# Half-width stationary operands by turns, two half steps to a burst, in a fused linear attention and two MoE layers

## The chip, the cores and the metric

One core of a Trainium2 chip runs the whole program in one launch. The metric is the time of one execution on the device in microseconds (us). The engines are TensorE (PE for its matmuls, PEld for its weight loads), VectorE (DVE), ScalarE (ACT), GpSimd (POOL) and SyncE (SP), which here issues the DMAs.

## The reference, cut to what matters

```python
# q, k, v: (4, 8, 576, 64); omega: (128, 64)
def phi(x):
    h = einsum('bhsd,md->bhsm', x, omega) - sum(x * x) / 2
    return exp(h - max(h)) / sqrt(m)
q_p, k_p = phi(q * scale), phi(k * scale)
kv  = einsum('bhsm,bhsd->bhmd', k_p, v)      # per batch and head: 128 x 64
z   = sum(k_p, axis=2)                       # per batch and head: 128
num = einsum('bhsm,bhmd->bhsd', q_p, kv)
den = einsum('bhsm,bhm->bhs', q_p, z) + 1e-6
x   = num / den                              # 2304 tokens x 512
x   = (silu(x @ w_gate) * (x @ w_val)) @ w_out          # d_ff 1536
out = x, and for the tokens that a skip score picks: x + gate * relu(x @ w1[e]) @ w2[e], 8 experts
```

## The kernel before, in words

The 2304 tokens are 18 tiles of 128 and 9 groups of 256. The attention is cut into half steps: 36 of kind "k" (they add to `kv` and `z`) and 36 of kind "q" (they make the numerators). A half step takes four (token tile, head) blocks. Two neighbouring tiles of one batch make a wide step (`w == 2`) of two heads each; tile 4 and tile 13 straddle two batches (576 tokens are 4.5 tiles) and are taken alone, in two runs of 64 tokens. The list `steps` has the k steps of the first nine tiles, the q steps of groups 0 to 3, then the k steps of the other nine tiles, and the q steps of groups 4 to 8.

Each half step begins in `phi` (line 301): two transposes (`tp`, line 329), the projection (`pj`: lines 345 to 347 up to step `first`, line 373 after it), sums and maxima on DVE, and four exponentials on ACT (line 396) into `pexp`, of which there are three buffers. A k step then runs four matmuls with `pexp` as the stationary operand, 128 columns wide, and 65 columns of `v` with a column of ones as the moving one (line 433, result `kvps` in PSUM). A q step transposes `pexp` (line 473), copies that to `qt` (line 477; three buffers), and runs four matmuls with `qt` stationary and 65 columns of `kv` moving (line 483, result `nm`). In the tiles 4 and 13 line 433 runs on 64 rows, twice, and line 483 on 64 columns, first all of one half and then all of the other. All of these are float32, and each stands in the trace as two pairs of a weight load and a matmul.

After `nm` come a reciprocal and a product on DVE (lines 492 to 497), two transposes (`tx`, line 510) and a split into a high and a low part (`xth`, `xtl`). `ups(g)` (line 669) multiplies a whole group by the first MoE's weights, `downs(g)` (lines 712 to 714) by the last of them. These two are the large part of TensorE's work, and they also fill it between the steps of the attention.

The order on every engine is made when the program is built. `Order` holds generators that each yield their next operation with an engine, a planned cost in ns, what it waits for, and which buffer slots it takes; the operation that can start first comes next, and the priority decides between equals. On the chip each engine runs its list in that order. Slots: six PSUM banks `a`, three `pexp`, three `g` (for `qt`), two buffers for `v` in the later half of the attention.

Of the kernel before, what the change touches and what calls it, by code (L numbers as in the profile page):

```python
# [9 lines left out]
F32 = mybir.dt.float32  # L10
# [40 lines left out]
def op(eng, ns, *after, take=()):  # L51

    return eng, ns, after, take


class Order:
# [26 lines left out]
    def rel(self, name, t, what=None):  # L83
        self.n += 1
        self.slots[name].append((t, self.n, what))
# [47 lines left out]
def tile_attn_moe_moe2(  # L133
# [90 lines left out]
    def runs(i, w):  # L224

        t0 = i * P
        if w == 2:
            yield 0, P, t0 // S, t0 % S
            return
        done = 0  # L230
        while done < P:
            b, s = divmod(t0 + done, S)
            n = min(P - done, S - s)
            yield done, n, b, s
            done += n

    def half_of(w, c):
        return c // 2 if w == 2 else c

    def head_of(w, c, u):  # L240

        return 2 * (c % 2) + u // 2 if w == 2 else u
# [34 lines left out]
    def give(name, buf, t):  # L277

        if late[name] and any(buf is b for b in aa + va):
            n_extra[0] -= 1  # L280
            if not n_extra[0]:
                rel("W", t)
        else:
            rel(name, t, buf)
# [36 lines left out]
    def phi(j, box, prio):  # L321

        yield op(None, 0, C["A", j])
        a = C["A", j].buf
        c_sq = od.add(square(a, C["A", j], box), prio)
        t = yield op("pe", 218, C["A", j], take=("a",))
        tp = ps_a.tile([P, 2, P], F32, tag="a", name="tp")
        for i in range(2):
            nc.tensor.transpose(tp[:, i, :], a[:, i, :], ident)
        od.add(give_later("A", a, t, c_sq))  # L330
        c_s = None
        if j < first:
            t = yield op("act", 264, t, take=("th",))
            tt = sp.tile([P, HH, P], F32R, tag="th", name="th")
            th, tl = tt[:, 0:2, :], tt[:, 2:4, :]
            nc.scalar.copy(th, tp)
            t = yield op("dve", 335, t)
            nc.vector.tensor_tensor(out=tl, in0=tp, in1=th.bitcast(F32), op=ALU.subtract)
            rel("a", t)
            c_s = od.add(sumsq(c_sq, box), prio)  # L340
            t = yield op("pe", 654, t, take=("a",))
            pj = ps_a.tile([P, HH, M], F32, tag="a", name="pj")
            for i in range(2):
                o = pj[:, 2 * i:2 * i + 2, :].rearrange("p h m -> p (h m)")
                nc.tensor.matmul(o, lhsT=th[:, i, :], rhs=omh, start=True, stop=False)
                nc.tensor.matmul(o, lhsT=tl[:, i, :], rhs=omh, start=False, stop=False)
                nc.tensor.matmul(o, lhsT=th[:, i, :], rhs=oml, start=False, stop=True)
            C["pj", j].t = t
            rel("th", t)
        else:  # L350

            ta, tl = [], []
            for r in range(2):
                ta.append((yield op("act", 264, t, take=() if r else ("th",))))
                if not r:
                    tt = sp.tile([P, 2, 2, P], F32R, tag="th", name="th")
                nc.scalar.copy(tt[rows[r], :, r, :], tp[rows[r]])  # L357
            for r in range(2):
                tl.append((yield op("dve", 335, ta[r])))
                nc.vector.tensor_tensor(  # L360
                    out=tt[rows[1 - r], :, r, :], in0=tp[rows[r]], in1=tt.bitcast(F32)[rows[r], :, r, :],
                    op=ALU.subtract,
                )
            rel("a", tl[1])
            c_s = od.add(sumsq(c_sq, box), prio)
            yield op(None, 0, take=("pexp",))
            box["pexp"] = sp.tile([P, HH, M], F32, tag="pe", name="pexp", bufs=3)
            td = []
            for i in range(2):
                t = yield op("pe", 218, *tl, C["omx"], take=("a",))  # L370
                pj = ps_a.tile([P, 2, 2, M], F32, tag="a", name="pj")
                for r in range(2):
                    nc.tensor.matmul(
                        pj[:, r].rearrange("p x m -> p (x m)"), lhsT=tt[:, i, r, :], rhs=omh, start=True, stop=True
                    )
                if i:
                    rel("th", t)
                td.append(od.add(halves(box, i, pj, t), prio))
            t = yield op(None, 0, *td)
            pj = box["pexp"]  # L380
        t = yield op("dve", 598, t, c_s)
        mx, mh, bi = (box["st"][:, i, :] for i in range(1, 4))
        nc.vector.tensor_reduce(out=mx, in_=pj, axis=AX.X, op=ALU.max)
        t = yield op("dve", 73, t, c_s)
        nc.vector.scalar_tensor_tensor(
            out=mh, in0=box["ssq"], scalar=-0.5 * scale * scale, in1=mx, op0=ALU.mult, op1=ALU.add
        )
        t = yield op("dve", 73, t)
        nc.vector.scalar_tensor_tensor(  # L389
            out=bi, in0=box["ssq"], scalar=-0.5 * scale * scale, in1=mh, op0=ALU.mult, op1=ALU.subtract  # L390
        )
        t = yield op("act", 1004, t, take=("pexp",) if j < first else ())
        if j < first:
            box["pexp"] = sp.tile([P, HH, M], F32, tag="pe", name="pexp", bufs=3)
        for h in range(HH):
            nc.scalar.activation(out=box["pexp"][:, h, :], in_=pj[:, h, :], func=ACTF.Exp, bias=bi[:, h:h + 1])  # L396
        if j < first:
            rel("a", t)
        rel("small", t)
        return t  # L400
# [14 lines left out]

    kvt = {}

    def kstep(j, prev, prio):
        _, i, w, c = steps[j]
        hf = half_of(w, c)  # L420
        box = {}
        t = yield from phi(j, box, prio)
        for off, n, b, s in runs(i, w):
            head = opens[b, hf] == j
            t = yield op("pe", 856, t, C["V", j], prev, take=("a",) if head else ())
            vt = C["V", j].buf
            if head:
                kvt[b, hf] = ps_a.tile([P, HH, D + 2], F32, tag="a", name="kvps")
            shares[b, hf] -= 1
            last = not shares[b, hf]  # L430
            for u in range(4):
                r = u % 2
                nc.tensor.matmul(
                    kvt[b, hf][:, head_of(w, c, u), r:r + D + 1], lhsT=box["pexp"][off:off + n, u, :],
                    rhs=vt[off:off + n, u // 2, r * (D + 1):(r + 1) * (D + 1)],
                    start=head and u == 0, stop=last, skip_group_check=True,
                )
            if last:
                od.add(kv_end(b, hf, t), 0, C["kv", b, hf])
        rel("pexp", t)  # L440
        give("V", vt, t)

    def kv_end(b, hf, t):

# [17 lines left out]
            C["xT", g].t = od.now  # L462

    def qstep(j, prio):
        _, i, w, c = steps[j]
        hf = half_of(w, c)
        part = list(runs(i, w))
        box = {}
        t = yield from phi(j, box, prio)
        t = yield op("pe", 436, t, take=("a",))  # L470
# [5 lines left out]
        qt = gp.tile([P, HH, P], F32, tag="g", name="qt")  # L476
        (nc.vector.tensor_copy if od.eng == "dve" else nc.scalar.copy)(qt, tq)
        rel("a", t)
        t = yield op("pe", 856 * len(part), t, *[C["kv", r[2], hf] for r in part], take=("a",))
        nm = ps_a.tile([P, HH, D + 1], F32, tag="a", name="nm")  # L480
        for off, n, b, s in part:
            for u in range(4):
                nc.tensor.matmul(
                    nm[off:off + n, u, :], lhsT=qt[:, u, off:off + n], rhs=kvs[b][hf][:, head_of(w, c, u), :],
                    start=True, stop=True,
                )
        rel("g", t)
        C["num", j].t = t
        t = yield op("dve", 69, t, take=("small",))
        dn = sm.tile([P, 2, HH], F32, tag="dn", name="dn")  # L490
        de, rd = (dn[:, i, :].rearrange("p (h o) -> p h o", o=1) for i in range(2))
# [31 lines left out]
    def attention():  # L523

        prev = Cell(0.0)
        live = []
        for j, (kind, i, _, _) in enumerate(steps):
            live = [c for c in live if c.t is None]
            if len(live) >= (MAXA if j < first else MAXB):
                yield op(None, 0, live[0])  # L530
                live.pop(0)
            yield op(None, 0, C["A", j], *([C["xT", i // 2]] if kind == "q" else []))
            prio = P_ATT if j < first else P_ATT2
            if kind == "k":
                prev = od.add(kstep(j, prev, prio), prio)
                live.append(prev)
            else:
                live.append(od.add(qstep(j, prio), prio, C["x", j]))
        for c in live:
            yield op(None, 0, c)  # L540

# [1059 lines left out]
```

## Time and profile before

| what | value |
|---|---|
| time before, median of 3 runs (lowest, highest) | 850.65 us (848.59, 850.86) |
| the profiled execution, its own time | 846.94 us |
| its span, first to last instruction | 844.7 us |
| TensorE busy with matmuls | 822.8 us, 97% |
| VectorE, ScalarE, GpSimd busy | 517.5, 446.0, 215.9 us |
| granted TensorE clock, mean | 0.995 of full speed |

The profile is of one execution. Busy times are unions: an engine counts once however many of its instructions are in progress. TensorE's matmuls overlap in the records, so that the price of a burst is read from the start of its first matmul to the start of the next one behind it, and not from the durations.

### The profile page before, as it was taken

What the parts mean: (1) busy time and instruction counts of PE and PEld (TensorE: products, weight loads), DVE (VectorE), ACT (ScalarE), POOL (GpSimd) and SP (SyncE); (2) the same over time, 40 slices, a digit from 0 to 9 for tenths busy, and PEclk for the clock granted to TensorE, in tenths of its full rate; (3) what the DMA queues carried; (4) which work ended last, traced back from release to release, by engine and by line L of the source; (5) the groups of instructions that cost most, each with busy time, mean ns of one, the idle gap of its engine ahead of it and who ended that gap; (6) DMA issues with size and microseconds to landing.
All of it is one profiled execution on the core that took longest, in us unless ns stands there. A gap on an engine that the chain in (4) does not pass through costs nothing. (4 is left out here: it accounts for less than half of the span.)

```text
span 844.7 us, 17205 instructions
## 1 busy us (share of the span) xinstructions
PE 822.8 (97%) x6221; PEld 778.4 (92%) x6221; DVE 517.5 (61%) x1477; ACT 446.0 (53%) x1162; POOL 215.9 (26%) x288
## 2 busy tenths in 40 slices
PE   9999999999999999999999999999999999999993
PEld 8989999999999899999999999999999999999993
DVE  7898777538877762652652651651475767846761
ACT  5897776437767662632632631631355447735560
POOL 4331231223222211211211212232151033342231
PEclk9999999999999999999999999999999999999997
DMA  6856862011222300200200200100185378657640
GB/s 165 234 169 192 249 201 76 1 57 31 53 66 54 95 14 1 70 7 1 75 3 1 75 2 1 63 1 1 52 236 153 117 230 262 218 171 243 200 129 31
DMA packets 77294, 84.46 MB, mean 100 GB/s; under 512 B 19550, under 2 KB 54494, under 8 KB 77200
## 3 DMA queue, kind: packets, MB, share of 16 engines
q1 hardware_dynamic: 73840, 76.23, 29.0%
q0 software_dynamic: 3360, 7.04, 2.8%
q8 instruction: 51, 0.84, 0.4%
q14 instruction: 43, 0.35, 0.1%
HBM read 71.48 MB, written 13.27 MB: 100 GB/s over the span
## 5 line engine op out<-in xcount | busy, mean ns | idle before, releaser
L669 PE MATMUL u<-xth,W 128*128 128x256 f32 x1728 | 247.1, 286 | 0.2 <-DVE h L690 0.2
L669 PEld LDWEIGHTS u<-xth,W 128*128 128x128 f32 x1728 | 225.3, 190 | 5.6 <-DVE h L690 0.4
L697 POOL TENSOR_TENSOR hl<-h,hh 128x256 fp32r<-128x256 f32 x108 | 82.9, 767 | 340.3 <-ACT hh L695 340.1
L669 PE MATMUL u<-xtl,W 128*128 128x256 f32 x864 | 138.8, 283 | 0.0
L669 PEld LDWEIGHTS u<-xtl,W 128*128 128x128 f32 x864 | 119.1, 192 | 0.0
L687 DVE SCALAR_TENSOR_TENSOR h<-h,u 128x256 f32<-128x256 f32 x108 | 45.3, 419 | 113.0 <-ACT h L685 112.4
L695 ACT CAST hh<-h 128x256 fp32r<-128x256 f32 x108 | 43.7, 405 | 116.3 <-DVE h L690 115.8
L690 DVE TENSOR_TENSOR h<-h,u 128x256 f32<-128x256 f32 x108 | 45.3, 419 | 75.5 <-PE u L669 74.8
L712 PE MATMUL y<-W,hh 128*128 128x512 f32 x216 | 87.4, 405 | 0.0
L685 ACT ACTIVATE h<-u 128x256 f32<-128x256 f32 x108 | 41.2, 382 | 83.2 <-PE u L669 81.2
L713 PE MATMUL y<-W,hh 128*128 128x512 f32 x216 | 85.1, 394 | 0.0
L714 PE MATMUL y<-W,hl 128*128 128x512 f32 x216 | 84.5, 391 | 0.0
L1107 DVE TENSOR_TENSOR W<-raw,W 128x512 fp32r<-128x512 f32 x107 | 72.6, 709 | 11.0 <-ACT W L1105 9.7
L1147 PE MATMUL hp<-xgt,W 128*128 128x288 f32 x546 | 76.2, 297 | 0.3 <-DVE W L1170 0.3
L1147 PEld LDWEIGHTS hp<-xgt,W 128*128 128x128 f32 x546 | 73.7, 188 | 0.9 <-DVE W L1170 0.5
L1105 ACT CAST W<-raw 128x512 fp32r<-128x512 f32 x112 | 65.1, 624 | 5.4 <-DMA raw<-in_moe_w_dram 5.3
L396 ACT ACTIVATE pexp<-pexp,st 128x128 f32<-128x128 f32 x184 | 58.8, 391 | 13.3 <-DVE st L389 13.0
L312 POOL TENSOR_TENSOR sq<-a 128x256 f32<-128x256 f32 x54 | 34.2, 632 | 72.8 <-DVE st L318 50.5
L1185 PE MATMUL ym<-W,W 128*128 128x288 f32 x168 | 52.1, 310 | 0.0
L360 DVE TENSOR_TENSOR th<-tp,th 64x256 fp32r<-64x256 f32 x92 | 38.9, 422 | 19.8 <-ACT th L357 17.7
L1187 PE MATMUL ym<-W,W 128*128 128x288 f32 x168 | 49.5, 295 | 0.0
L1186 PE MATMUL ym<-W,W 128*128 128x288 f32 x168 | 49.5, 295 | 0.0
(217 smaller groups left out, 1521.5 us busy)
## 6 DMA issues: line engine op xcount, KB each, us to landing
raw<-in_moe_w_dram SPq DMA_DIRECT2D x64, 512.0 KB, 4.7
scratch<-in_moe_w_out_dram SPq DMA_DIRECT2D x11, 511.8 KB, 3.9
scratch<-in_moe_w_gate_dram SPq DMA_DIRECT2D x11, 511.0 KB, 4.6
scratch<-in_moe_w_val_dram SPq DMA_DIRECT2D x11, 511.0 KB, 4.1
x2s<-x SPq DMA_DIRECT2D x9, 512.0 KB, 2.6
out_dram<-x SPq DMA_DIRECT2D x9, 512.0 KB, 4.0
a<-in_q_dram SPq DMA_DIRECT2D x26, 128.0 KB, 2.2
a<-in_k_dram SPq DMA_DIRECT2D x22, 128.0 KB, 2.3
```

Source lines behind the costliest of these rows:

```text
L396: nc.scalar.activation(out=box["pexp"][:, h, :], in_=pj[:, h, :], func=ACTF.Exp, bias=bi[:, h:h + 1])
L669: nc.tensor.matmul(ps, lhsT=W[fc][:, 2 * n + wi, c * P:(c + 1) * P], rhs=x[:, c, :], start=(a == 0 and c == 0), stop=(a == 2 and c == 3),)
L697: nc.gpsimd.tensor_tensor(out=hl, in0=h, in1=hh.bitcast(F32), op=ALU.subtract)
L712: nc.tensor.matmul(y[n], lhsT=hh[:, s], rhs=W[fc][:, 4, :], start=(fc == 0), stop=False)
L713: nc.tensor.matmul(y[n], lhsT=hh[:, s], rhs=W[fc][:, 5, :], start=False, stop=False)
L714: nc.tensor.matmul(y[n], lhsT=hl[:, s], rhs=W[fc][:, 4, :], start=False, stop=(fc == NFC - 1))
L1105: nc.scalar.copy(blk(m, b, 0), raw[:, j, :])
L1107: (nc.vector if od.eng == "dve" else nc.gpsimd).tensor_tensor(out=blk(m, b, 1), in0=raw[:, j, :], in1=blk(m, b, 0).bitcast(F32), op=ALU.su ...
L1147: nc.tensor.matmul(hp[:, 0:TS], lhsT=blk(m, (fc // 4) * 4 + c, wi)[:, fs], rhs=m2["xt"][xi][:, c, :], start=(a == 0 and c == 0), stop=(a = ...
L1185: nc.tensor.matmul(y, lhsT=wh, rhs=hh, start=(fc == 0), stop=False)
L1186: nc.tensor.matmul(y, lhsT=wl, rhs=hh, start=False, stop=False)
L1187: nc.tensor.matmul(y, lhsT=wh, rhs=hl, start=False, stop=(fc == 7))
```

## The change

Three things change, all in the attention.

First, every 65-column matmul with a stationary operand of 128 columns becomes two, of columns 0 to 63 and 64 to 127 (`rows` holds the two slices), which write partitions 0 to 63 and 64 to 127 of the same PSUM tile. The two stand next to each other, so that the halves come by turns. In tiles 4 and 13 the k matmuls, cut in row halves already, are cut in columns as well, and the q matmuls get the order by turns.

Second, half steps get a mate: two k steps next to each other of one half of the heads, or two q steps of one tile or pair of tiles. The first of the two stops behind its `pexp` (k) or its `qt` (q) and keeps the buffer; the second issues the matmuls of both in one burst. Of 36 k half steps 32 have a mate; all 36 q half steps have one. What follows `nm` becomes a generator of its own (`numer`), started for both.

Third, the planner is told of it: one operation of 1250 ns for a burst of two half steps, or 800 for one, and `pexp` buffers are taken in the order of the steps (`C["px", j]`).

```diff
+    mate = {j: j for j in range(len(steps))}
+    for j in range(1, len(steps)):
+        (kind, i, w, c), (kind2, i2, w2, c2) = steps[j - 1:j + 1]
+        if mate[j - 1] == j - 1 and kind == kind2 and (half_of(w, c) == half_of(w2, c2) if kind == "k" else i == i2):
+            mate[j - 1], mate[j] = j, j - 1
...
     def kstep(j, prev, prio):
         t = yield from phi(j, box, prio)
-        for off, n, b, s in runs(i, w):
-            t = yield op("pe", 856, t, C["V", j], prev, take=("a",) if head else ())
...
+        C["ft", j].t, C["ft", j].buf = t, box["pexp"]
+        if mate[j] > j:
+            return
+        both = sorted({j, mate[j]})
+        t = yield op(
+            "pe", 1250 if len(both) == 2 else 800, *[C[x, n] for x in ("ft", "V") for n in both], prev,
+            take=("a",) * sum(r[-1] for n in both for r in parts[n]),
+        )
+        for n in both:
...
             for u in range(4):
                 r = u % 2
-                nc.tensor.matmul(
-                    kvt[b, hf][:, head_of(w, c, u), r:r + D + 1], lhsT=box["pexp"][off:off + n, u, :],
+                for off, num, b, _, head in parts[n]:
+                    for m in rows:
+                        nc.tensor.matmul(
+                            kvt[b, hf][m, head_of(w, c, u), r:r + D + 1], lhsT=pexp[off:off + num, u, m],
...
     def qstep(j, prio):
+        C["qt", j].t, C["qt", j].buf = t, qt
+        if mate[j] > j:
+            return
...
+            for u in range(4):
+                for m, b in at:
+                    nc.tensor.matmul(
+                        nm[m, u, :], lhsT=qt[:, u, m], rhs=kvs[b][half_of(w, c)][:, head_of(w, c, u), :],
+                        start=True, stop=True,
+                    )
+            od.add(numer(n, nm, t), prio, C["x", n])
```

TensorE's order at the first bursts of k steps, before (`x4` counts the kernel's matmuls; `v_103`, `v_104` and `extra` are buffers of v, `a_105`, `a_106` and `extra` of k):

```order
L347 MATMUL pj<-oml,th 128x256
L433 MATMUL kvps<-v_104,pexp 128x65 x4
L329 MATMUL tp<-ident,extra 128x128 x2
L329 MATMUL tp<-ident,a_105 128x128 x2
L433 MATMUL kvps<-extra,pexp 128x65 x4
L329 MATMUL tp<-ident,a_106 128x128 x2
L433 MATMUL kvps<-extra,pexp 128x65 x4
L345 MATMUL pj<-omh,th 128x256
```

The same place now:

```order
L347 MATMUL pj<-oml,th 128x256
L452 MATMUL kvps<-v_103,pexp 64x65 x8
L452 MATMUL kvps<-v_104,pexp 64x65 x8
L329 MATMUL tp<-ident,a_105 128x128 x2
L345 MATMUL pj<-omh,th 128x256
L346 MATMUL pj<-omh,th 128x256
L347 MATMUL pj<-oml,th 128x256
L345 MATMUL pj<-omh,th 128x256
L346 MATMUL pj<-omh,th 128x256
L347 MATMUL pj<-oml,th 128x256
L452 MATMUL kvps<-extra,pexp 64x65 x16
```

The matmuls of two half steps stand together, twice as many and half as wide, and a projection stands ahead of the second burst that stood behind it.

TensorE's order at the first q steps, before:

```order
L473 MATMUL tq<-ident,pexp 128x128 x8
L510 MATMUL tx<-ident,xx 128x128 x2
L483 MATMUL nm<-kv_1_108,qt 128x65 x4
L510 MATMUL tx<-ident,xx 128x128 x2
L329 MATMUL tp<-ident,extra 128x128 x2
L473 MATMUL tq<-ident,pexp 128x128 x4
L483 MATMUL nm<-kv_1_108,qt 128x65 x4
L510 MATMUL tx<-ident,xx 128x128 x2
L483 MATMUL nm<-kv_0_107,qt 128x65 x4
L473 MATMUL tq<-ident,pexp 128x128 x4
L345 MATMUL pj<-omh,th 128x256
```

The same place now:

```order
L490 MATMUL tq<-ident,pexp 128x128 x8
L512 MATMUL nm<-kv_0_107,qt 64x65 x16
L490 MATMUL tq<-ident,pexp 128x128 x4
L512 MATMUL nm<-kv_1_108,qt 64x65 x16
L544 MATMUL tx<-ident,xx 128x128 x2
L512 MATMUL nm<-kv_0_107,qt 64x65 x16
L544 MATMUL tx<-ident,xx 128x128 x2
L329 MATMUL tp<-ident,extra 128x128 x2
L544 MATMUL tx<-ident,xx 128x128 x4
```

Three bursts now stand within six rows, with no projection among them: those of the next steps have moved ahead of this place.

## Rows read from the trace of the kernel before

**Rows 1.** The page: span; busy us of each engine (share), x instructions.
```profile
span 844.7 us, 17205 instructions
PE 822.8 (97%) x6221; PEld 778.4 (92%) x6221; DVE 517.5 (61%) x1477; ACT 446.0 (53%) x1162; POOL 215.9 (26%) x288
```

**Rows 2.** Stretches, us: length, busy time by engine (x instructions), clock, DMA share, GB/s.
```profile
0.00:45.00 45.00, 42.85 (x352) 40.96 (x352) 35.59 (x127) 33.03 (x106) 17.07 (x41) 1.00 0.73 201
45.00:62.20 17.20, 15.36 (x125) 13.73 (x124) 17.20 (x59) 17.20 (x50) 5.95 (x6) 1.00 0.53 161
62.20:85.00 22.80, 22.80 (x178) 21.98 (x178) 20.13 (x48) 17.89 (x43) 3.37 (x4) 1.00 0.60 185
85.00:566.00 481.00, 480.05 (x3627) 449.90 (x3626) 281.76 (x870) 249.99 (x680) 109.53 (x149) 1.00 0.17 53
566.00:800.00 234.00, 231.42 (x1717) 221.79 (x1716) 143.47 (x339) 113.00 (x253) 69.81 (x78) 1.00 0.53 168
```

**Rows 3.** PE's waits from 85 to 566: us in total, times, longest.
```profile
PE rk L822 <- DVE th L360: 0.3, 1, 0.3
```

**Rows 4.** Instruction groups of PE, 0 to 85: busy us, mean ns, idle before.
```profile
L433 PE MATMUL kvps<-extra,pexp 128*128 128x65 f32 x80 | 10.1, 270 | 0.5 <-ACT pexp L396 0.5
L483 PE MATMUL nm<-kv,qt 128*128 128x65 f32 x64 | 8.3, 273 | 0.3 <-ACT qt L477 0.2
L433 PE MATMUL kvps<-v,pexp 128*128 128x65 f32 x48 | 6.1, 270 | 0.0
L433 PE MATMUL kvps<-extra,pexp 64*128 64x65 f32 x32 | 4.4, 278 | 0.0
```

**Rows 5.** The same view, 85 to 566.
```profile
L483 PE MATMUL nm<-kv,qt 128*128 128x65 f32 x192 | 24.5, 271 | 0.0
L433 PE MATMUL kvps<-v,pexp 128*128 128x65 f32 x128 | 16.3, 270 | 0.0
L433 PE MATMUL kvps<-v,pexp 64*128 64x65 f32 x32 | 4.4, 278 | 0.0
L483 PE MATMUL nm<-kv,qt 128*64 128x65 f32 x64 | 3.9, 227 | 0.0
```

**Rows 6.** PE in order of time, a burst of 128 columns: start, length (us).
```profile
66.72 1.00 PE L483 MATMUL nm<-kv,qt 128*128 128x65 f32 x8
67.53 0.37 PE L669 MATMUL u<-xth,W 128*128 128x256 f32 x1
```

**Rows 7.** PE in order of time, a burst on 64 rows.
```profile
35.70 0.28 PE L347 MATMUL pj<-oml,th 128*128 128x256 f32 x1
35.91 1.10 PE L433 MATMUL kvps<-extra,pexp 64*128 64x65 f32 x8
36.95 0.38 PE L345 MATMUL pj<-omh,th 128*128 128x256 f32 x1
```

**Rows 8.** PE in order of time, the burst of 64 columns of tile 4.
```profile
140.92 0.52 PE L669 MATMUL u<-xtl,W 128*128 128x256 f32 x3
141.37 0.97 PE L483 MATMUL nm<-kv,qt 128*64 128x65 f32 x16
142.27 0.33 PE L748 MATMUL tpr<-ident,x 128*128 128x128 f32 x1
```

**Rows 9.** Weight loads of line 483 in progress (x) in stretches of 0.12 us.
```profile
141.42:141.54 0.12, 0.12 (x4) 1.00 0.00 0
...
141.66:141.78 0.12, 0.12 (x8) 1.00 0.00 0
141.78:141.90 0.12, 0.12 (x8) 1.00 0.00 0
...
66.84:66.96 0.12, 0.12 (x3) 1.00 0.00 0
```

**Rows 10.** Group 4's last transposes; matmuls of line 669 by then (x).
```profile
L510 PE MATMUL tx<-ident,xx x8: 271/272/277, 304.9 to 315.3; 128*128 128x128 f32 x8
...
0.00:315.50 315.50, 134.83 (x1021) 1.00 0.37 111
```

More of the change, by code (lines that the diff above doesn't have):

```diff
@@ L365, in phi @@
             c_s = od.add(sumsq(c_sq, box), prio)
-            yield op(None, 0, take=("pexp",))
+            yield op(None, 0, *([C["px", j - 1]] if j else []), take=("pexp",))
+            C["px", j].t = 0.0
             box["pexp"] = sp.tile([P, HH, M], F32, tag="pe", name="pexp", bufs=3)
@@ L391, in phi @@
         )
-        t = yield op("act", 1004, t, take=("pexp",) if j < first else ())
+        t = yield op("act", 1004, t, *([C["px", j - 1]] if 0 < j < first else []), take=("pexp",) if j < first else ())
         if j < first:
+            C["px", j].t = 0.0
             box["pexp"] = sp.tile([P, HH, M], F32, tag="pe", name="pexp", bufs=3)
@@ L416, in tile_attn_moe_moe2 @@
     kvt = {}
+    mate = {j: j for j in range(len(steps))}
[3 more added lines that the diff above has]
+            mate[j - 1], mate[j] = j, j - 1
     def kstep(j, prev, prio):
-        _, i, w, c = steps[j]
-        hf = half_of(w, c)
         box = {}
         t = yield from phi(j, box, prio)
-        for off, n, b, s in runs(i, w):
-            head = opens[b, hf] == j
-            t = yield op("pe", 856, t, C["V", j], prev, take=("a",) if head else ())
[L426 to L430, printed above, removed]
+        C["ft", j].t, C["ft", j].buf = t, box["pexp"]
+        if mate[j] > j:
+            return
+        both = sorted({j, mate[j]})
+        parts = {n: [(*r, opens[r[2], half_of(*steps[n][2:])] == n) for r in runs(*steps[n][1:3])] for n in both}
+        t = yield op(
[3 more added lines that the diff above has]
+        for n in both:
+            _, _, w, c = steps[n]
+            hf = half_of(w, c)
+            vt, pexp = C["V", n].buf, C["ft", n].buf
+            for _, _, b, _, head in parts[n]:
+                if head:
+                    kvt[b, hf] = ps_a.tile([P, HH, D + 2], F32, tag="a", name="kvps")
+                shares[b, hf] -= 1
@@ L431, in kstep @@
             for u in range(4):
                 r = u % 2
-                nc.tensor.matmul(
-                    kvt[b, hf][:, head_of(w, c, u), r:r + D + 1], lhsT=box["pexp"][off:off + n, u, :],
[L435 to L441, printed above, removed]
+                for off, num, b, _, head in parts[n]:
+                    for m in rows:
+                        nc.tensor.matmul(
+                            kvt[b, hf][m, head_of(w, c, u), r:r + D + 1], lhsT=pexp[off:off + num, u, m],
+                            rhs=vt[off:off + num, u // 2, r * (D + 1):(r + 1) * (D + 1)],
+                            start=head and u == 0, stop=not shares[b, hf], skip_group_check=True,
+                        )
@@ L443, in kv_end @@
+            for _, _, b, _, _ in parts[n]:
+                if not shares[b, hf]:
+                    od.add(kv_end(b, hf, t), 0, C["kv", b, hf])
+            rel("pexp", t)
+            give("V", vt, t)
     def kv_end(b, hf, t):
@@ L464, in qstep @@
     def qstep(j, prio):
-        _, i, w, c = steps[j]
-        hf = half_of(w, c)
-        part = list(runs(i, w))
         box = {}
@@ L478, in qstep, with numer @@
         rel("a", t)
-        t = yield op("pe", 856 * len(part), t, *[C["kv", r[2], hf] for r in part], take=("a",))
-        nm = ps_a.tile([P, HH, D + 1], F32, tag="a", name="nm")
-        for off, n, b, s in part:
-            for u in range(4):
[L483 to L488, printed above, removed]
+        C["qt", j].t, C["qt", j].buf = t, qt
+        if mate[j] > j:
+            return
+        both = sorted({j, mate[j]})
+        t = yield op(
+            "pe", 1250 if len(both) == 2 else 800, *[C["qt", n] for n in both],
+            *[C["kv", r[2], half_of(*steps[n][2:])] for n in both for r in runs(*steps[n][1:3])],
+            take=("a",) * len(both),
+        )
+        for n in both:
+            _, i, w, c = steps[n]
+            nm, qt = ps_a.tile([P, HH, D + 1], F32, tag="a", name="nm"), C["qt", n].buf
+            at = [(m, b) for off, num, b, _ in runs(i, w) for m in rows if off <= m.start < off + num]
+            for u in range(4):
+                for m, b in at:
+                    nc.tensor.matmul(
+                        nm[m, u, :], lhsT=qt[:, u, m], rhs=kvs[b][half_of(w, c)][:, head_of(w, c, u), :],
+                        start=True, stop=True,
+                    )
+            rel("g", t)
+            C["num", n].t = t
+            od.add(numer(n, nm, t), prio, C["x", n])
+    def numer(j, nm, t):
+        _, i, w, c = steps[j]
+        hf = half_of(w, c)
         t = yield op("dve", 69, t, take=("small",))
@@ L534, in attention @@
             if kind == "k":
-                prev = od.add(kstep(j, prev, prio), prio)
-                live.append(prev)
-            else:
-                live.append(od.add(qstep(j, prio), prio, C["x", j]))
+                live.append(od.add(kstep(j, prev, prio), prio))
+                if mate[j] <= j:
+                    prev = live[-1]
+            else:
+                od.add(qstep(j, prio), prio)
+                live.append(C["x", j])
         for c in live:
```

## The prediction

> **What bounds the kernel now.** I read the page's totals first, then busy time by stretches, then the waits, then the bursts themselves in order of time. TensorE is busy for 822.8 of 844.7 us [rows 1], so the question is where it is the limit and where it only looks so. The stretches answer that [rows 2]. From 85 to 566 us it is busy for 480.05 of 481.00 us while DVE stands at 59%, and one wait of 0.3 us is all that it has there [rows 3]: in this stretch every us taken from TensorE's list is a us of the kernel, as long as the list behind it is ready. From 566 to 800 it is busy for 231.4 of 234 us with no attention left in it; the instructions of every engine from the end of the attention on stand in the same order as before, so this part and what comes after it should only move. The first 85 us are another matter. From 45 to 62 DVE and ACT are busy all of the time (17.20 of 17.20) and TensorE is not (15.36); from 0 to 45 DVE has 35.59 of 45 and TensorE 42.85; from 62 to 85 TensorE is full again, with DVE at 20.13 of 22.80. There DVE and ACT are close behind TensorE or ahead of it. The granted clock is 1.00, the 2.4 GHz level, in all five stretches, so it enters neither side of the sum.
>
> **What the change removes.** A burst of four matmuls with 128 columns stands as eight pairs of load and matmul, and takes 0.81 us from its first matmul to the next one behind it [rows 6]. A burst on 64 rows takes longer for the same count: the matmul ahead of it starts at 35.70, 0.12 later the burst could start, it starts at 35.91, and the next one stands at 36.95, so its place is 1.13 us. A whole half step of tile 4 as 64 columns, one half behind the other, has sixteen pairs: three matmuls 0.12 apart from 140.92 on would put it at 141.28, the next one stands at 142.27, so its place is 0.99 us [rows 7, 8].
>
> The counts are the x of the groups over eight (over sixteen for the 64-column ones). From 85 to 566 [rows 5]: 24 + 16 full bursts, 4 on 64 rows, 4 of 64 columns: 40 x 0.81 + 4 x 1.13 + 4 x 0.99 = 32.4 + 4.5 + 4.0 = 40.9 us. From 0 to 85 [rows 4]: (80 + 48) / 8 + 64 / 8 = 24 full ones and 4 on 64 rows: 19.4 + 4.5 = 23.9 us.
>
> **What it adds.** The new bursts need two prices: one for each pair of 64 columns when the halves come by turns, one for going into this form and out of it. No burst of before takes turns, but the one of tile 4 passes from one half to the other in its middle, and there the trace shows both halves at once: in 0.12 us four weight loads are in progress while one half runs, and eight in the 0.24 us around the change-over; a burst of 128 columns has three [rows 9]. So two halves can run side by side, and the pace doubles.
>
> For the size I take the price of the form from the burst on 64 rows, which has the same number of pairs as a full one: 1.13 - 0.81 = 0.32, call it 0.30. The burst of tile 4 then leaves 0.69 us for its sixteen pairs, of which a third at double pace. With s for one pair alone, 0.46 / s + 0.23 x 2 / s = 16, so s = 0.057 us alone, and 0.029 by turns. A burst of two half steps has 32 pairs: 0.30 + 32 x 0.029 = 1.23 us. One of the four k steps without a mate: 0.30 + 16 x 0.029 = 0.76. A pair with a half step of tile 4 or 13 among the k steps has 32 pairs of a quarter of the array and 16 of a half, and one more change of form (0.09, what the way into tile 4's burst cost, 141.37 against 141.28): 0.39 + 48 x 0.029 = 1.78. The other end of the form's price is those 0.09 alone; then s is 0.061, and the burst of two 0.09 + 32 x 0.031 = 1.08. I take 1.23, since the bursts on 64 rows show the whole price, in and out.
>
> From 85 to 566 there are 6 + 14 bursts of two, 2 with a straddling tile, 2 alone: 24.6 + 3.6 + 1.5 = 29.7 us. Saved: 40.9 - 29.7 = 11.2 us, all of it on the engine that sets the end. From 0 to 85: 6 + 4 bursts of two, 2 and 2: 12.3 + 3.6 + 1.5 = 17.4 us, saved on TensorE 23.9 - 17.4 = 6.5 us.
>
> The Trainium skill, "TensorE: Matmul & The Clock Gate", "Part 3: Packing small matmuls — row/col tiling", speaks against the doubled pace: a weight load overlaps matmuls in flight only where its row group is another one, and two column halves share theirs. By that rule the 32 pairs would cost 0.057 each and the burst 2.12 us instead of 1.23. Rows 9 show otherwise for 0.24 us.
>
> **What holding back costs.** The first half step of each two waits for the second: its `pexp` or `qt` stays taken, two of three buffers, and `nm` comes later. From 85 to 566 this is hidden by the first MoE's matmuls. When the last transposes of group 4 are done at 315.3, 1021 of the 1152 matmuls of groups 0 to 3 are issued [rows 10]; 131 are left, at 0.12 us some 16 us of filling. A step of the attention may come that much later before TensorE has nothing to do; the change takes about 6 us of TensorE's own work out of the part up to there, so 10 are left, against a hold-back of one half step. If that cover were gone, TensorE would stop for what is missing, since its order is fixed. DVE and ACT have the room (59% and 52% busy there).
>
> From 0 to 85 the cover is thin. Of the 6.5 us, 5.0 lie in the k steps up to 45 us. DVE has 9.4 us idle there; 5.0 less would put it at 35.6 of 40, 89%. I count 3 of them. The 1.5 of the q steps lie where DVE and ACT are full, and I count none. The bounds: all 6.5, or a loss, if each of the 14 bursts there now waits as line 433 (0.5) and line 483 (0.3) did once or more [rows 4]: 10 x 0.5 + 4 x 0.3 = 6.2 us of new waits, against the 3 counted a net loss of 3.2.
>
> **The sum.** 11.2 + 3.0 = 14.2 us. The profiled execution took 846.94 us, 2.2 more than its span and 3.7 less than the median of the runs, 850.65; the difference is taken off the median: 836.5 us.
>
> **The rivals.**
> - The halves don't keep side by side. Place: every burst; price: a pair at 0.057 instead of 0.029. 768 pairs from 85 to 566 then cost 21.5 us more, a loss of 10.3 there; 448 pairs before cost 12.5 more, a loss of 6.0. It gives 866.9 us, slower. It decides from 0.044 us a pair on, where the saving is gone (11.2 / 768 = 0.015 over 0.029). For it: the doubled pace was seen for 0.24 us alone, at a change-over and not under turns; tile 4's burst as a whole ran at 0.69 / 16 = 0.043. Against it: eight loads in progress in both of these stretches.
> - The pace is kept in part, 0.036 a pair, between the two. The saving from 85 to 566 falls to 5.8 us, the early one to about 1.5: 843.3 us.
> - Holding back costs the early part its gain and 3.2 us: 11.2 - 3.2 = 8.0 us, 842.7 us. For it: DVE and ACT at 100% from 45 to 62, and three bursts of q steps that stand nearly together, with no projection among them to fill TensorE. Against it: the projections that stood there are not gone but done earlier, so TensorE has the same work before the first MoE begins.
> - The early part gains all of its 6.5 us: 17.7, 833.0 us. For it: DVE's 9.4 us of idle time.
> - The saving is lost wholly in new waits elsewhere, from 848 to 853 us: the one wait of 0.3 us in 481 speaks against it.
>
> **How the numbers follow.** Forecast 0.50, pace in part 0.18, early loss 0.08, all of the early gain 0.12: all of these are faster by over 0.3%, that is under 848.1 us, which is about what a measurement of this kernel can tell from no change. Halves one behind the other 0.08, slower. Saving lost elsewhere 0.04, no change. Together 0.88 faster, 0.04 same, 0.08 slower. The range goes from 829 us (all of the early gain, and a form that costs nearer 0.09 than 0.30: 34 x 0.15 = 5.1 us at most on top of 833.0) to 846 us (pace and early loss together); the slower rival is left out of it.
>
> **What would show it.** In the profile after: some eight weight loads of a burst in progress in 0.12 us all through it, and 1.1 to 1.3 us from its first matmul to the next behind it; about 1.8 for the four with a straddling tile; TensorE still without waits between the first MoE's start and the last attention step, that stretch shorter by some 11 us and all behind it moved; TensorE's idle time before the first matmul of line 669's kind larger than now, by about half of the work taken out there. Four or five loads in progress and 2 us a burst would make the prediction wrong, and so would waits for `pexp` or `qt` between 85 and 566.

## The result, and the profile after

The changed kernel takes 839.37 us in the median of 4 runs (835.86 to 843.1); the kernel before, run beside it, 850.33. The ratio is 0.987, interval 0.9834 to 0.9905: 11.0 us less, where 14.2 were forecast. The profiled execution took 842.22 us, with a span of 840.4. The page's totals, in the form of [rows 1]:

```profile
span 840.4 us, 18356 instructions
PE 805.1 (96%) x6797; PEld 752.5 (90%) x6797; DVE 517.6 (62%) x1477; ACT 447.7 (53%) x1162; POOL 214.9 (26%) x288
```

TensorE is busy for 17.7 us less. That this is to the tenth what the prediction took out of its list (11.2 + 6.5) is chance: the bursts shrank by more than that, as shown below, and 10.2 us of this execution (6.8 from 29.9 on, 3.4 from 562.4 on) ran at the 1.2 GHz level, the granted clock 0.50. The span is only 4.3 us shorter: 13.4 us are new idle time. Both profiles are of one execution each, before of a quick one (846.94 us, median 850.33) and after of a long one (842.22), so the two spans understate the change. The stretches say where it lies; columns as in [rows 2], with the same bounds:

```profile
0.00:45.00 45.00, 38.26 (x487) 33.84 (x489) 33.60 (x125) 31.02 (x101) 15.72 (x41) 0.92 0.67 188
45.00:62.20 17.20, 14.52 (x199) 12.31 (x195) 14.69 (x52) 16.57 (x52) 6.02 (x6) 1.00 0.50 136
62.20:85.00 22.80, 21.30 (x178) 19.04 (x177) 20.54 (x51) 17.33 (x40) 3.11 (x3) 1.00 0.52 158
85.00:566.00 481.00, 475.47 (x4044) 441.37 (x4043) 288.83 (x883) 256.72 (x692) 115.23 (x164) 1.00 0.18 56
```

TensorE's idle time is 6.74 us in the first 45 us (2.15 before), 4.18 from 45 to 85 (1.84 before), and 5.53 from 85 to 566 (0.95 before). In the first row the granted clock is 0.92, and DVE has got less done than before (33.60 against 35.59 us).

The bursts are what the forecast hung on. TensorE in order of time (start, length), the three kinds of burst, each between its neighbours, to be read as [rows 6 to 8]:

```profile
13.20 0.28 PE L347 MATMUL pj<-oml,th 128*128 128x256 f32 x1
13.41 1.16 PE L452 MATMUL kvps<-v,pexp 128*64 128x65 f32 x32
14.50 0.44 PE L329 MATMUL tp<-ident,a 128*128 128x128 f32 x2
...
25.07 0.28 PE L347 MATMUL pj<-oml,th 128*128 128x256 f32 x1
25.28 0.69 PE L452 MATMUL kvps<-v,pexp 128*64 128x65 f32 x16
25.89 0.44 PE L329 MATMUL tp<-ident,extra 128*128 128x128 f32 x2
...
242.45 0.64 PE L705 MATMUL u<-xtl,W 128*128 128x256 f32 x4
243.02 1.31 PE L452 MATMUL kvps<-v,pexp 64*64 64x65 f32 x48
244.26 0.74 PE L374 MATMUL pj<-omh,th 128*128 128x256 f32 x4
```

A burst of two half steps runs 1.09 us to the next matmul, and starts 0.09 later than a matmul 0.12 behind its forerunner would: 1.18 us for its place (forecast 1.23). Alone it is 0.61 + 0.09 = 0.70 (0.76). With a straddling tile it is 1.24 + 0.09 = 1.33 (1.78). Of the 30 bursts of two, 28 took 1.08 to 1.09; the other two stand at half the clock (1.93) and ahead of a wait (1.42). Of the four straddling ones, three took 1.24 and the first 1.54. The weight loads of line 452 in progress (x), in stretches of 0.12 us at the start, the middle and the end of the first burst, answer [rows 9]:

```profile
13.50:13.62 0.12, 0.12 (x8) 1.00 1.08 269
13.80:13.92 0.12, 0.12 (x8) 1.00 1.00 295
14.10:14.22 0.12, 0.12 (x8) 1.00 0.94 184
```

The eight loads that stood at a change-over for 0.24 us now stand nearly all through. Two matmuls, one of each half, start 0.007 us apart, and the next two about 0.058 behind them.

The new waits are in two places. TensorE's waits from 0 to 85 us and from 85 to 566 (us, times, longest), against [rows 3 and 4]:

```profile
PE pj L345 <- ACT pexp L398: 3.2, 1, 3.2
PE pj L345 <- DVE th L338: 3.0, 5, 0.8
PE tq L490 <- ACT pexp L398: 1.3, 3, 0.7
PE tx L544 <- DVE xx L531: 1.3, 2, 1.0
...
PE u L705 <- DVE h L726: 3.5, 3, 2.5
PE u L705 <- DVE h L723: 1.0, 1, 1.0
```

The longest, on TensorE and on ACT in order of time:

```profile
27.19 0.38 PE L329 MATMUL tp<-ident,a 128*128 128x128 f32 x2
30.79 0.58 PE L345 MATMUL pj<-omh,th 128*128 128x256 f32 x1 [3.22 <-ACT pexp L398]
...
28.97 0.78 ACT L657 ACTIVATE top<-scratch 128x512 f16<-128x512 bf16 x1 [2.18 <-DMA scratch<-in_moe_w_val_dram]
29.62 1.11 ACT L398 ACTIVATE pexp<-pj,st 128x128 f32<-128x128 f32 x4
```

ACT's order has a piece of a first-MoE weight (line 657) ahead of the next exponentials; the piece lands late, ACT stands 2.18 us, the exponentials come behind it, and TensorE's projection, which needs the bank that they read, stands 3.22 us. From 29.9 to 36.7 the granted clock is 0.50, and the burst in it took 1.93 us instead of 1.09.

The other place is at 558 us, on DVE and POOL:

```profile
557.54 0.42 DVE L554 TENSOR_TENSOR xtl<-tx,xth 128x256 fp32r<-128x256 f32 x1
557.88 4.34 DVE L929 TENSOR_SCALAR nix<-c 128x64 f32<-128x64 f32 x1
558.38 3.83 DVE L726 TENSOR_TENSOR h<-h,u 128x256 f32<-128x256 f32 x1
...
557.45 4.26 POOL L933 MEMSET xg<- 96x512 f32 x9
561.65 0.52 POOL L933 MEMSET sxg<- 64x512 f32 x1
```

A small product of the second MoE's preparation (`nix`) lasts 4.34 us, to 562.2, until the ten memsets are done; `h` of the first MoE is queued behind it, and TensorE waits 2.5 us for that `h`, and from 562.4 on the granted clock is 0.50 for 3.4 us. In the kernel before the same product stands as far behind the start of the same memsets (0.43 us) and took 0.61 us:

```profile
567.10 0.61 DVE L893 TENSOR_SCALAR nix<-c 128x64 f32<-128x64 f32 x1
...
566.67 4.31 POOL L897 MEMSET xg<- 96x512 f32 x9
570.93 0.52 POOL L897 MEMSET sxg<- 64x512 f32 x1
```

### The profile page after: what moved, and what is told of

Read it like the earlier page. It is cut to its first block, busy times and chain, and to the rows that moved or that the text cites. A ratio compares the mean times of both kernels' runs of the same rounds, so it can differ in the third digit from the quotient of the medians.

```text
span 840.4 us, 18356 instructions
## 1 busy us (share of the span) xinstructions
PE 805.1 (96%) x6797; PEld 752.5 (90%) x6797; DVE 517.6 (62%) x1477; ACT 447.7 (53%) x1162; POOL 214.9 (26%) x288
## 4 chain that ended last, share of the span: by engine, by line
PE 78%; DVE 6%; DMA 6%; ACT 4%; issue 2%; POOL 1%; SPq 1%; ACTq 0%; POOLq 0%; DVEq 0%
PE u L705 32%; PE hp L1183 7%; PE y L748 5%; PE y L749 5%; PE y L750 5%; PE ym L1221 3%; PE pj L374 3%; PE ym L1223 3%; PE ym L1222 3%; PE nm L512 2%; DMA scratch<-in_moe_w_val_dram 2%; ACT pexp L398 2%; PE tq L490 1%; DMA scratch<-in_moe_w_gate_dram 1%; PE tp L329 1%
## 5 line engine op out<-in xcount | busy, mean ns | idle before, releaser
L705 PE MATMUL u<-xth,W 128*128 128x256 f32 x1728 | 250.0, 287 | 4.7 <-DVE h L726 3.5
L726 DVE TENSOR_TENSOR h<-h,u 128x256 f32<-128x256 f32 x108 | 48.7, 451 | 62.4 <-PE u L705 60.8
L750 PEld LDWEIGHTS y<-W,hl 128*128 128x128 f32 x216 | 40.7, 189 | 10.2 <-POOL hl L733 0.9
```

The source lines that it names most:

```text
L705: nc.tensor.matmul(ps, lhsT=W[fc][:, 2 * n + wi, c * P:(c + 1) * P], rhs=x[:, c, :], start=(a == 0 and c == 0), stop=(a == 2 and c == 3),)
L750: nc.tensor.matmul(y[n], lhsT=hl[:, s], rhs=W[fc][:, 4, :], start=False, stop=(fc == NFC - 1))
```

## The experiments

Each was timed beside the kernel before (medians 850.0, 851.7 and 851.2 us in the three series). "First MoE" is the start of the first matmul of `ups(0)`: 62.2 us before, 66.0 after. It differs between executions of one order: 63.0 in a second profile of the early order of before (`e10_before_nix`), and 64.7, 65.6 and 64.2 in three more of the changed one (`e8_after_again`, `e3_nix_on_act`, `e11_nix_again`).

**Halves by turns alone** (`e1_turns_alone`): the kernel before with its own order, and only the matmuls cut.

```diff
-                nc.tensor.matmul(kvt[b, hf][:, ...], lhsT=box["pexp"][off:off + n, u, :], ...)
+                for m in rows:
+                    nc.tensor.matmul(kvt[b, hf][m, ...], lhsT=box["pexp"][off:off + n, u, m], ...)
...
```

> The kernel before with its order untouched; only the 65-column matmuls become halves by turns, no half step is held back. Theory A (the halves side by side are the gain, holding two half steps only saves one change of form): a half step falls from 0.81 to 0.71 us, as the four k steps without a mate show in the changed kernel; a q step of tile 4 from 0.99 to 0.71, a run of 64 rows from 1.13 to about 0.65. From 85 to 566 us that is 40 x 0.10 + 4 x 0.28 + 4 x 0.48 = 7.0 us, before it about 2 of 4.3: some 841 us. Theory B (the gain needs the pair, since a change of form eats what one half step saves): within 2 us of the kernel before, 849 to 851.

Measured: 846.56 us, ratio 0.9954 (0.9931 to 0.9976). A burst takes 0.61 us, with the way in 0.70, as expected, but the kernel gains only 3.5 us, which lies between the two theories. The first MoE begins at 63.1 us, so the work taken out ahead of it brought nothing, and TensorE has new waits from 85 to 566; the three largest:

```profile
PE pj L373 <- DVE th L360: 1.0, 2, 0.6
PE lp L762 <- DVE x2t L756: 0.8, 3, 0.4
PE pj L373 <- ACT h L687: 0.5, 1, 0.5
```

**Holding back alone** (`e2_pairs_alone`): the changed kernel with whole 128-column operands.

```diff
...
-                    for m in rows:
+                    for m in (slice(0, P),):
...
```

> Two half steps to a burst as in the change, but at the full width of 128 columns (and in row runs for tiles 4 and 13), planned at 856 a half step. Theory A (holding back is hidden behind the first MoE from 85 us on and costs the first 85 us something): nothing saved on TensorE but 2 to 6 us lost before 85 us: 852 to 856 us. Rival (holding back costs nothing): 849 to 851 us. If holding back itself also saved time: below 848.

Measured: 856.58 us, ratio 1.0063 (1.004 to 1.0086): 6.6 us slower than before. The first MoE begins at 69.7, 7.5 us late. The two largest waits of the first 85 us, and all from 85 to 566:

```profile
PE kvps L452 <- ACT pexp L398: 2.8, 2, 2.1
PE pj L345 <- DVE th L338: 2.0, 4, 0.9
...
PE pj L374 <- DVE th L360: 0.9, 2, 0.6
PE u L705 <- DVE h L723: 0.5, 1, 0.5
```

From the start of group 0's `ups` to that of group 8's it takes 528.4 us, and 528.1 before: where first-MoE matmuls cover it, holding back costs nothing to speak of. Part of the early 7.5 us is the clock's, which is 0.50 from 20.9 us on for 6.8; how much was not told apart. Behind group 8's start it loses 2.7 us more (257.1 against 254.4 to the end).

**No turns** (`e4_no_turns`): the changed kernel, all of one half and then all of the other.

```diff
...
-            for u in range(4):
-                for m, b in at:
+            for m, b in at:
+                for u in range(4):
```

> The changed kernel with the same matmuls in the same bursts, but in each half step all of columns 0 to 63 first and then all of 64 to 127, as tile 4's q steps stood before the change. Theory A (turns are what puts two halves side by side): a pair at about 0.043 us as in tile 4's old burst, 1.5 us a burst of two instead of 1.17: 34 x 0.35 = 12 us more, about 851. Rival (the two halves run side by side in any order, the reordering of loads finds them): within 2 us of the changed kernel, 838 to 841.

Measured: 851.29 us, ratio 1.0009 (0.9986 to 1.0033): 12 us back, all of the gain, though the order of steps is that of the changed kernel on every engine. The same burst of two, here 1.48 us to the next matmul and not 1.09, and its weight loads in progress, first within one half and then at the first change-over:

```profile
13.21 1.55 PE L452 MATMUL kvps<-v,pexp 128*64 128x65 f32 x32
14.69 0.44 PE L329 MATMUL tp<-ident,a 128*128 128x128 f32 x2
...
13.27:13.39 0.12, 0.12 (x4) 1.00 0.92 239
13.51:13.63 0.12, 0.12 (x8) 1.00 0.56 145
```

The first MoE begins at 65.4, as it does with turns (64.2 to 66.0): the longer bursts ahead of it cost nothing there.

**The small product on ScalarE** (`e3_nix_on_act`, and once more as `e11_nix_again`): the changed kernel with one instruction moved.

```diff
-        nc.vector.tensor_scalar_mul(m2["nix"], m2["c64"], -1.0 / 128)
+        nc.scalar.activation(out=m2["nix"], in_=m2["c64"], func=ACTF.Copy, scale=-1.0 / 128)
```

> The changed kernel; one 128x64 product (nix, the kernel's line 929), which took 4.34 us on VectorE beside ten GpSimd memsets and 0.61 us in the kernel before, is made on ScalarE instead. Theory A (this product was held until the memsets had ended, TensorE stood 2.5 us for the VectorE instruction behind it, and its clock was at 1.2 GHz for the next 3.4 us): the wait and the low clock near 562 us are gone, 4 us less where it happened, so a median of 835 to 837 and fewer slow runs. Rival (the 6 us between the runs of the changed kernel come from the first 85 us): median 838 to 840 as before, the spread as wide.

> The changed kernel with the small product on ScalarE, once more, beside the two others. Its first time was 836.96 us, ratio 0.9835. Theory A: the stall beside the memsets is worth 2 to 3 us, and the ratio comes out from 0.982 to 0.985 again, under the change's 0.9856 and 0.987. Theory B: the stall is hidden by work behind it, and the ratio is that of the change, 0.986 or 0.987.

Measured: 836.96 us, ratio 0.9835 (0.9801 to 0.9869), and then 838.06, ratio 0.9835 (0.98 to 0.9869). `h` of line 726 takes 0.42 us beside the memsets again, and the wait of 2.5 us is gone; one of 1.2 us stands near its place, for GpSimd's `hl`, which comes behind the memsets on that engine. The intervals overlap those of the changed kernel, so that the 2 to 3 us rest on the profile and on two agreeing medians.

**The changed kernel again** (`e8_after_again`).

> The changed kernel again, untouched, beside the three others, so that its spread and its median are known from the same chip and hour. Theory A of the product on VectorE (held beside the memsets in a part of the runs): median 838 to 840, two clusters some 4 us apart, the lower one at the median of the kernel with the product on ScalarE, 837. Rival (that stall is not what spreads the runs): the median within 1 us of 837.

Measured: 839.36 us, ratio 0.9856 (0.9823 to 0.9889). Both stalls are there again: 3.7 us for `pexp` early, 2.5 for the `h` behind the product, and `nix` lasts 4.34 us; the first MoE begins at 64.7. The median is that of the first theory, but its two clusters are not there: the six runs spread from 837.1 to 843.6.

**The same move in the kernel before** (`e10_before_nix`).

> The kernel before with the small product on ScalarE, and nothing else. Theory A: the product only costs where GpSimd's memsets stand beside it, and in the kernel before it took 0.61 us: no difference, ratio 1.000 within 0.002. Theory B: moving it is worth something by itself, about 2 us (ratio 0.9975), and the gain of that edit in the changed kernel is no stall's.

Measured: 852.52 us, ratio 1.0009 (0.9983 to 1.0035). No difference: in this kernel, where the product had taken 0.61 us, the edit is worth nothing. Up to the start of group 8's `ups` TensorE's order is that of the kernel before, so its profile (an execution of 850.07 us) is a second one to compare with: first MoE at 63.0, and 529.7 us from the start of group 0's `ups` to that of group 8's.

**A later landing in the plan** (`e5_late_landing`): the small product on ScalarE, and the weights' pieces planned to land 3500 ns behind their issue, not 950.

```diff
-            C["raw", j].t = t + 950
+            C["raw", j].t = t + 3500
...
```

> The changed kernel with nix on ScalarE, and the planner told that a piece of the first MoE's weights lands 2.55 us later than it assumed (3500 ns behind the issue's own 1456 instead of 950). Theory A (TensorE's wait of 3.2 us from 27.6 to 30.8 us, and the 1.2 GHz clock behind it, come from a conversion in ScalarE's list that stands ahead of the exponentials and waits for its DMA, planned to land 2.4 us after its issue where the trace shows 5.1): that wait is gone, 3 to 5 us less than with nix alone: 832 to 834. Rival (DVE and ACT are simply full there, the wait moves to the next step): 836 to 838.

Measured: 841.92 us, ratio 0.9893 (0.9859 to 0.9927): a miss. The early wait is gone and the first MoE begins at 60.8, 4.8 us sooner than without this edit; but from the start of group 1's `ups` to group 3's it takes 153.5 us (141.1 without it), and from group 0's to group 8's 522.5 (514.8). TensorE's largest waits from 85 to 566:

```profile
PE tx L544 <- DVE xx L531: 2.1, 2, 1.6
PE pj L374 <- DVE th L360: 1.3, 5, 0.4
PE pj L374 <- DVE pexp L409: 1.2, 3, 0.6
PE y L750 <- POOL hl L733: 1.2, 1, 1.2
```

The edit changes the whole order behind it; which of its moves makes these waits was not tried.

**Turns alone, told to the planner** (`e6_turns_planned`): the first experiment with 710 ns instead of 856 for a burst.

> Halves by turns without holding back, as in the first experiment, but planned at 710 ns a burst instead of 856, so that the order fits the shorter bursts. Theory A (the first experiment gave 3.5 us instead of 9 because TensorE, early at every step, met waits for VectorE and ScalarE that the old order had placed for longer bursts): 842 to 844. Rival (one half step saves too little and the early part is bound elsewhere, whatever the order): 846 to 847.

Measured: 848.94 us, ratio 0.9967 (0.995 to 0.9985): a miss, not better than without. The first MoE begins at 66.1 instead of 63.1.

**No k step held early** (`e7_late_pairs`): the small product on ScalarE; the first 18 k steps run alone, planned at 710.

```diff
-        if mate[j - 1] == j - 1 and kind == kind2 and (...):
+        if (kind == "q" or j > first) and mate[j - 1] == j - 1 and kind == kind2 and (...):
...
```

> The changed kernel with nix on ScalarE, and without holding back among the first 18 k steps (there each half step issues its own halves by turns, planned at 710). Theory A (holding back costs the first 45 us, where nothing fills TensorE): 2 to 4 us less than with nix alone, 833 to 835. Rival (the early loss is the wait behind a weight piece, which has nothing to do with holding back): 836 to 838, or worse by the changes of form that the early pairs saved, 0.5 us each for 8 pairs at most.

Measured: 843.36 us, ratio 0.9895 (0.9868 to 0.9923): a miss. The first MoE begins at 70.5. The two things that this kernel still had early are the 710 (66.1 in the experiment above) and the held q steps, so the last one took both away.

**No step held before the first MoE** (`e9_hold_after_first`): the 8 q steps ahead of it run alone too, planned at 856 as before, and early `pexp` buffers are no longer taken in the order of the steps; the small product stays on ScalarE.

```diff
-        if mate[j - 1] == j - 1 and kind == kind2 and (...):
+        if j > first and mate[j - 1] == j - 1 and kind == kind2 and (...):
...
```

> Halves by turns everywhere, but no half step is held back before the first MoE has begun (the 18 k steps and 8 q steps ahead of it run one to a burst, as in the kernel with turns alone); behind that all are held as in the change; the small product on ScalarE. Theory A: the early loss of the change comes of holding back where nothing covers it, so the first MoE begins at about 63 us, as with turns alone, the rest goes as in the kernel that only moves the product (66.0), and the time is about 834 us, 3 under that kernel run beside it. Theory B: what is won before the first MoE is lost behind it again, as it was with the late landing, since the second half of the attention then meets engines that are not ready: first MoE at 63, and a time within 1.5 us of that kernel, 837.

Measured: 834.79 us, ratio 0.9786 (0.9754 to 0.9819): the first theory, and the fastest kernel here. The slowest of its five runs (835.04) is quicker than the quickest of the six of `e11_nix_again` beside it (835.71). The first MoE begins at 63.1. Its first stretches, and TensorE's larger waits from 85 to 566:

```profile
0.00:45.00 45.00, 39.67 (x495) 33.70 (x496) 34.28 (x125) 31.21 (x103) 15.80 (x41) 1.00 0.70 194
45.00:62.20 17.20, 14.69 (x172) 11.79 (x170) 17.20 (x58) 17.20 (x51) 6.72 (x7) 1.00 0.55 161
...
PE y L778 <- POOL hl L761: 1.2, 1, 1.2
PE tx L571 <- DVE xx L558: 0.5, 1, 0.5
```

The clock is 1.00 up to 822 us; DVE and ACT are full from 45 to 62 as in [rows 2], where the changed kernel had DVE at 14.69 of 17.20.

## Why the prediction was right, and where it was not

**The time** is inside the range and 2.9 us above the forecast, which is in part luck: the sum was off in its two terms in opposite directions, and it had no term for two smaller losses.

**TensorE sets the end from 85 to 566: right.** From the start of group 0's `ups` to that of group 8's it takes 528.1 us before (529.7 in the second profile of that order), 517.8 and 517.2 in the two profiles after, and 513.8 in the fastest kernel. With the measured prices the new bursts from 85 to 566 cost 20 x 1.18 + 2 x 1.33 + 2 x 0.70 = 27.7 us. Those of before, taken place by place (from 0.12 us behind the matmul ahead to the matmul behind), cost 42.5 us: the prediction's 40.9 priced every full burst at 0.81, but about half of them take 0.83 or more, by what stands next to them. So 14.8 us were saved, where 11.2 were forecast; 10.3 to 12.5 of it reached the start of group 8, and 14.3 or more did in the fastest kernel.

**The pace: right, and the mechanism is shown.** Turns undone, in the same order, cost the whole gain, and the burst of two has its place in 1.18 us. Two pairs by turns every 0.058 us are the 0.029 a pair of the forecast; what was priced too high is the form, at 0.30 us instead of 1.18 - 32 x 0.029 = 0.25. By the rule of the Trainium skill that was weighed ("TensorE: Matmul & The Clock Gate", "Part 3: Packing small matmuls — row/col tiling"), that a weight load overlaps only where its row group is another one, it would have been 2.12 us; the trace does not agree for column halves. The straddling burst was priced too high for a reason that the runs show: its 48 pairs take 1.24 / 48 = 0.026 each, those of a burst of halves 1.09 / 32 = 0.034. In its first part four quarters of the array start together, where the forecast had two.

**The rival was not what happens without turns.** It put a pair of one half alone at 0.057 us, and so 866.9 us. Within one half the kernel without turns does start its matmuls about 0.058 us apart, with four loads in progress. But wherever one half gives way to the other, both run side by side there too (eight loads), three times in a burst of two: it takes 1.48 / 32 = 0.046 a pair, and the kernel 851.29 us. The prediction had read such a change-over in the burst of tile 4 ([rows 9]) and left it out of the rival's price.

**The first 85 us: this is the step that failed.** The prediction counted 3.0 us of gain ("I count 3 of them") out of 6.5 that TensorE loses in work. Measured: the first MoE begins 3.8 us later (2.5 in the second profile; against 63.0, the second profile of the early order of before, 3.0 and 1.7). Two parts of that are told apart. First, work taken from TensorE brought nothing as long as the order stayed: turns alone keep the order of before and begin the first MoE at 63.1, where that order begins it at 62.2 and 63.0, and the changed order begins it at 65.4 without turns and at 64.2 to 66.0 with them. DVE and ACT were full from 45 to 62, and TensorE's idle time ahead of the first MoE grew by 4.0 us instead (3.99 before, 8.02 in the fastest kernel). Second, the order with held steps costs 1 to 3 us more; held at full width it costs 7.5. The rival "holding back costs the early part its gain and 3.2 us", given 0.08, had this place and nearly this size.

What the argument "DVE has 9.4 us of idle time" left out is that an engine's idle time in a stretch is no room, as long as its next operand comes from an engine further round the circle: TensorE waits for ACT's exponentials and DVE's `th`, which wait for TensorE's transposes and projections. That a held burst lengthens that round is argued and not shown. All four profiles of the held order with turns have TensorE's wait of 3.0 to 3.7 us for the exponentials behind a weight piece; the kernels that hold nothing early don't have it, and nor does the one with the later landing, which holds its steps too and begins the first MoE at 60.8, sooner than any. So the early loss belongs to this planned order, and no run shows that holding back must cost it.

**TensorE without waits between the first MoE and the last attention step: nearly.** From 85 to 566 there are 2.6 us of waits (0.3 of them for `pexp`, which the prediction named as a sign against it) beside the one of 2.5 behind the product, for which it had no term. "This part and what comes after it should only move" was true of the order and not of the durations. The product beside the memsets went from 0.61 to 4.34 us; moving it took the ratio from 0.9856 and 0.987 to 0.9835, some 2 to 3 us. And from the start of group 8's `ups` to the end it takes 254.4 us before (255.2 in the second profile) and 256.7 and 256.6 after: 1.4 to 2.3 us lost, whose cause was not looked for.

**How the parts go together.** Turns alone are worth 3.5 us, holding alone costs 6.6, both gain 11 to 12. With steps held, halves without turns are 5.3 us better than full width (856.58 to 851.29; the plan for full width is longer, so the orders differ), and the turns bring 12 more, in one order. Place by place, the bursts with turns alone save 42.5 - 35.1 = 7.4 us from 85 to 566; from group 0's `ups` to group 8's 3.5 came through, and the waits from 85 to 566 come to 2.8. Held in pairs the same work saves 14.8, since two half steps cost 1.18 us in one burst and 1.40 in two, and the waits other than that behind the product are about the same, 2.6. Held only where first-MoE matmuls stand to fill the time, and with the product on ScalarE, the two gain 16.4 us (851.19 to 834.79).

What stays open: why a landing planned later, which mends the early part, loses more behind it; and why the product is held by the memsets in one kernel and not in another, for which the last section has a sign.

## What to carry to other kernels

Cut a stationary operand of 128 columns with few moving ones into halves and let them come by turns; with steps held, one half behind the other stood 5 us better than the full width here, halves by turns 17. Collect such bursts where the engine has other work to fill the wait; leaving the start of this kernel, where each engine waits for the next, with one step at a time was worth 3 us (834.79 against 838.06). When a change only shortens a list, look at what the moved instructions stand beside: a trace of before tells their durations only for the neighbours that they had.

## What the runs showed of the hardware that was not expected

- A DVE product of 128x64 float32 beside ten memsets of GpSimd lasted 4.34 us in two profiles of the changed kernel, and about as long in the kernels with holding alone and with no turns (4.33); it took 0.61 us in the kernel before and with turns alone, and 2.42 in the one with turns planned, although it began 0.43 to 0.49 us behind the first memset in all of them. The `h` of line 726 behind it took 3.83 us instead of 0.42. The Trainium skill, "SBUF — State Buffer", section "Who interferes with whom", says that an operation of this kind (`tensor_scalar`) can run in a mode in which it and GpSimd block each other, and that who issues first holds the ports for its whole instruction. The trace agrees that it waits (to 562.2, where the last memset ends at 562.17), but it waited for all of the memsets left and not for one. One thing goes with it in all seven profiles: where the product was long (4.3 and 2.42 us), `h` was ready and its record starts 0.45 to 0.51 us behind the product's start, before the product's end; where it took 0.61 us, DVE then stood idle for 1.3 us. Without the product in front, the same `h` took 0.42 us beside the memsets. Whether the instruction behind is the cause was not tried.
- Quarters of the array run more side by side than halves: a burst of 48 pairs, 32 of them quarters, took 1.24 us (1.54 for the first one), one of 32 halves 1.09. Four quarters start within 0.02 us and the next four about 0.058 behind the first, as two halves do.
- The granted clock fell to 0.50 (1.2 GHz) near TensorE's longest stands, and not each time alike. In one profile of the changed kernel it fell at 29.9, 2.4 us into the stand of 3.22 us, and stayed for 6.8 us; the burst in it took 1.93 us. In the other it fell at 32.2, some 1.5 us after a stand of 3.67 us had ended, and stayed for 3.4. The stand of 2.5 us behind the product was followed by 3.4 us at 0.50 in the first profile and by none in the second.
